# Feed-forward weight transfers kept in program order, each gate and up set issued one group ahead, the first down tiles spread over the last groups

## The chip, the cores and the metric

The kernel runs on one core of one Trainium2 chip. The metric is device time in microseconds (us), the median of several executions. The span of a profile, from its first to its last instruction, is about 1.8 us shorter than the time of the same execution. PE is the matmul engine, DVE the vector engine, ACT the scalar engine, and SP the engine from whose queue the loads are issued.

## The reference

One transformer block with conditioning. The six vectors sa, ca, ga, sb, cb, gb come from `silu(c) @ w_mod`.

```python
h = _layernorm(x, axis=-1) * (1 + ca) + sa
x = x + ga * _A_ref(h, A_k_cache, A_v_cache, A_wq, A_wo)   # attention, 32 heads, last 512 cached keys
h = _layernorm(x, axis=-1) * (1 + cb) + sb
x = x + gb * _B_ref(h, B_w_gate, B_w_up, B_w_down)         # (silu(h@w_gate) * (h@w_up)) @ w_down
```

There are 2048 rows of 1024 values, and the feed-forward width is 3584. Everything is bf16.

## The kernel before

Attention comes first, then the feed-forward part (FFN) in four blocks of 512 rows. A block has seven groups of gate and up products (four units of 16 matmuls each), then two halves of down products. Both kernels hand their instructions to a scheduler, which may reorder each engine's stream by its own estimate. `pin` marks an instruction that it must leave at its place in the program; `stage` says which kinds are pinned. `at(k, ...)` sets a task beside step k.

The names in the views: `xn` is a normalised tile of 128 rows, `hT` holds the transposed rows, which the affine steps then scale and shift. `gu_ps` is the PSUM tile (PSUM is where matmuls accumulate) of one gate and up unit, `sg` the silu of its gate half, and `guT` the product of the two halves; once `guT` is done, the `gu_ps` buffer is free. `d_ps`, `a_ps`, `q_ps` and `s_ps` are the PSUM tiles of the down, output, query and score products. `wg`, `wu` and `wd` are weight tiles; `v_sb` is also the spare weight buffer.

```python
    pb_ = ctx.enter_context(tc.tile_pool(name="blkB", bufs=7))    # gate and up tiles, 512 KB each
    pc_ = ctx.enter_context(tc.tile_pool(name="blkC", bufs=12))   # wo and down tiles
    ...
    stage = {"dma": True, "steps": False}

    def pin(ins, what="steps"):
        return tc.keep_in_program_order(ins) if stage[what] else ins

    def fetch(out, in_):
        pin(nc.sync.dma_start(out=out, in_=in_), "dma")
    ...
    def load_cols(n, k, dst, add_one):           # scale and shift as columns (modT)
        ...
            fetch(out=dst, in_=src)
        if add_one:
            nc.vector.tensor_scalar(out=dst, in0=dst, scalar1=1.0, scalar2=None, op0=ALU.add)
    ...
    def ln_norm(tt, on_act=False):
        mv = ln.pop(tt)
        n = wk.tile([P, D], BF16, name="xn", tag="xn", bufs=3)
        ...
            pin(nc.vector.tensor_scalar(out=n, in0=xt[tt], scalar1=mv[:, 0:1],
                                        scalar2=mv[:, 2:3], op0=ALU.subtract, op1=ALU.mult))
    ...
    def ln_xpose(key, tt):                       # DMA transpose, hT<-xn, on SP's queue
        ...
        pin(nc.sync.dma_start_transpose(
            out=hT[key][:, :, t * P:(t + 1) * P], in_=xn.pop(tt)), "dma")

    def ln_affine(key, dt, ps, sc, sh, on_act):  # eight of these after the four transposes
        ...
            pin(nc.vector.tensor_scalar(out=hT[key][:, dt, :], in0=ps, scalar1=sc[:, dt:dt + 1],
                                        scalar2=sh[:, dt:dt + 1], op0=ALU.mult, op1=ALU.add))
    ...
    def emit_gu(cc, f):
        ...
        ps = big("gu_ps")                        # two PSUM buffers
        ...                                      # 8 gate and 8 up matmuls
        nc.scalar.activation(out=g, in_=ps[:, 0, :], func=ACT.Silu)
        nc.vector.tensor_tensor(out=guT[(cc, fg)][:, fi, :], in0=ps[:, 1, :], in1=g, op=ALU.mult)
    ...
    stage.update(dma=False, steps=False)         # from here the scheduler orders the loads
    for cc in range(NTC):
        for fg in range(NFG):
            if (cc, fg) != (0, 0):
                load_gu(cc, fg)
            if cc > 0:
                load_wd(cc, 0, fg)
            for fi in range(4):
                emit_gu(cc, 4 * fg + fi)
                run_tasks(NU + 1 + (cc * NFG + fg) * 4 + fi)
        for dh in range(DH):
            if dh > 0 or cc == 0:
                for fg in range(NFG):
                    load_wd(cc, dh, fg)
            for t in range(QT):
                ...
                emit_down(cc, dh, t, (256, 128, 128) if last else (512,))
```

Of the kernel before, what the change touches and what calls it, by code (L numbers as in the profile page):

```python
# [588 lines left out]
def fast_path(ctx, tc, flag, A_x, A_k_cache, A_v_cache, A_wq, A_wo, B_x, B_w_gate, B_w_up,  # L589
# [14 lines left out]
    NTC = S // TCW  # L604
# [7 lines left out]
    NFG = FT // 4  # L612
# [30 lines left out]
    def blkB(name, shape, dt=BF16):  # L643
        return pb_.tile(shape, dt, name=name, tag="B")

    def blkC(name, shape, dt=BF16):
        return pc_.tile(shape, dt, name=name, tag="C")
# [10 lines left out]
    stage = {"dma": True, "steps": False}  # L658
# [7 lines left out]
    def load(out, in_):  # L666
        with nc.allow_non_contiguous_dma(reason="weight slice"):
            fetch(out=out, in_=in_)
# [157 lines left out]
# [3 lines that stand above are left out]
        if on_act:  # L829
            nc.vector.scalar_tensor_tensor(out=mv[:, 3:4], in0=mv[:, 0:1], scalar=-1.0,  # L830
                                           in1=mv[:, 2:3], op0=ALU.mult, op1=ALU.mult)
            nc.scalar.activation(out=n, in_=xt[tt], func=ACT.Identity, bias=mv[:, 3:4],
                                 scale=mv[:, 2:3])
        else:
            pin(nc.vector.tensor_scalar(out=n, in0=xt[tt], scalar1=mv[:, 0:1],
                                        scalar2=mv[:, 2:3], op0=ALU.subtract, op1=ALU.mult))
        return n
# [85 lines left out]
    for t in range(QT):  # L923
        ln_stats(t)
        n = ln_norm(t, t % 2 == 0)
# [128 lines left out]
    def emit_o(g):  # L1054
        cc, h = divmod(g, H)
        kv = h // rep
        if h % 4 == 0:
            oq[(cc, h // 4)] = blkC("oq", [P, QT, 4, Dh])
        for t in range(QT):
            if o_slot["n"] == 0:  # L1060
                o_slot["ps"] = mm("o_ps", (P, SLOTS, VN))
            s_ = o_slot["n"]
            for j in range(WT):
                nc.tensor.matmul(o_slot["ps"][:, s_, :], lhsT=pT[g][:, j, t * P:(t + 1) * P],  # L1064
                                 rhs=v_sb[:, kv, j, 0:VN], start=(j == 0),
                                 stop=(j == WT - 1))
            runs = o_slot["runs"]
            if runs and runs[-1][0] == g:
                runs[-1][2] = t + 1
            else:  # L1070
                runs.append([g, t, t + 1, s_])
            o_slot["n"] = s_ + 1
            if o_slot["n"] == SLOTS or (t == QT - 1 and h % HQ == HQ - 1):
                close_bank()
        del pT[g]
# [46 lines left out]
    for tt in range(QT, S // P):  # L1122
        cc, t = divmod(tt, QT)
# [33 lines left out]
    def load_gu(cc, fg):  # L1157

        for nm, v in (("wg", wg_v), ("wu", wu_v)):
            for i in range(2):  # L1160
                spare = (cc * NFG + fg) % 2 == 1 and nm == "wu" and i == 1
                t = v_blk if spare else blkB(nm, [P, 4, 512])
                load(t, v[:, 4 * i:4 * i + 4, fg * 512:(fg + 1) * 512])
                gu_w[(cc, fg, nm, i)] = t

    def emit_gu(cc, f):
        fg, fi = divmod(f, 4)
        if fi == 0:
            guT[(cc, fg)] = blkA("guT", [P, 4, TCW])
        ps = big("gu_ps")  # L1170
        for n, nm in enumerate(("wg", "wu")):
            for dt in range(DT):
                nc.tensor.matmul(ps[:, n, :],  # L1173
                                 lhsT=gu_w[(cc, fg, nm, dt // 4)][:, dt % 4, fi * P:(fi + 1) * P],
                                 rhs=hT[("h2", cc)][:, dt, :], start=(dt == 0),
                                 stop=(dt == DT - 1))
        g = wk.tile([P, TCW], BF16, name="sg", tag="row", bufs=5)
        nc.scalar.activation(out=g, in_=ps[:, 0, :], func=ACT.Silu)  # L1178
        nc.vector.tensor_tensor(out=guT[(cc, fg)][:, fi, :], in0=ps[:, 1, :], in1=g, op=ALU.mult)  # L1179

    def load_wd(cc, dh, fg):
        t = blkC("wd", [P, 4, 512])
        load(t, wd_v[:, 4 * fg:4 * fg + 4, dh * 512:(dh + 1) * 512])
        wd_tiles[(cc, dh, fg)] = t

    def emit_down(cc, dh, t, widths=(512,)):
        row = (cc * QT + t) * P
        c0 = 0
        for w in widths:
            dsl = slice(dh * 512 + c0, dh * 512 + c0 + w)  # L1190
            d_ps = mm("d_ps", (P, w))
            for f in range(FT):
                nc.tensor.matmul(d_ps, lhsT=guT[(cc, f // 4)][:, f % 4, t * P:(t + 1) * P],  # L1193
                                 rhs=wd_tiles[(cc, dh, f // 4)][:, f % 4, c0:c0 + w],
                                 start=(f == 0), stop=(f == FT - 1))
            r = wk.tile([P, w], FP32, name="f32", tag="f32", bufs=2)
            nc.vector.tensor_tensor(out=r, in0=d_ps, in1=gb_bc[:, dsl], op=ALU.mult)  # L1197
            o = wk.tile([P, w], BF16, name="o_sb", tag="row", bufs=5)
            nc.vector.tensor_tensor(out=o, in0=r, in1=xt[cc * QT + t][:, dsl], op=ALU.add)
            nc.scalar.dma_start(out=out2d[row:row + P, dsl], in_=o)  # L1200
            c0 += w

    def run_tasks(k):
        for f, a in tasks.pop(k, ()):
            f(*a)

    stage["steps"] = True
    for k in range(NU + 1):
# [9 lines left out]
        run_tasks(k)  # L1218
        if k >= 1:
            emit_o(k - 1)  # L1220
    stage.update(dma=False, steps=False)
    for cc in range(NTC):
        for fg in range(NFG):
            if (cc, fg) != (0, 0):
                load_gu(cc, fg)
            if cc > 0:
                load_wd(cc, 0, fg)
            for fi in range(4):
                emit_gu(cc, 4 * fg + fi)
                run_tasks(NU + 1 + (cc * NFG + fg) * 4 + fi)  # L1230
        for dh in range(DH):
            if dh > 0 or cc == 0:
                for fg in range(NFG):
                    load_wd(cc, dh, fg)
            for t in range(QT):
                last = cc == NTC - 1 and dh == DH - 1 and t == QT - 1
                emit_down(cc, dh, t, (256, 128, 128) if last else (512,))
# [3 lines left out]
def kernel(tc, *args):  # L1241
    nc = tc.nc
    with tc.tile_pool(name="guard", bufs=1) as gp:
        flag = gp.tile([1, 1], I32, name="flag")
        fast_path(tc, flag, *args)
        over = nc.values_load(flag[0:1, 0:1], min_val=0, max_val=1)
        with tc.If(over > 0):
            general_path(tc, *args)
# [30 lines left out]
```

## Time and profile before

| | |
|---|---|
| time, three runs | 1283.59 us median (1283.0 to 1285.08) |
| time of the profiled run, and its span | 1284.75 us, 1283.0 us |
| PE without a matmul | 13.0 us of the span |
| transfers | 204.21 MB, 159 GB/s over the span |

The prediction below shows the lines that carry its argument. Two more are wanted as a yardstick. They are from the timeline of PE in the kernel before (start, length, engine, line, what): the first gate matmul of the FFN and the first down matmul. The count that ends a line is that of the matmuls merged into it inside the view's window, so a window's end can cut it.

```profile
675.45 1.89 PE L1173 MATMUL gu_ps<-hT,wg 128*128 128x512 bf16 x8
...
793.86 2.32 PE L1193 MATMUL d_ps<-wd,guT 128*128 128x512 bf16 x10
```

Between these two starts lie 28 units of 16 matmuls and 12 output projections of 8, together 544. At the pace of 96.69 / 448 = 0.2158 us they need 117.41 us; the kernel before took 793.86 - 675.45 = 118.41. This stretch holds all that the change can win, while whole executions of one kernel differ by 2 us.

The other small loss in the middle of the kernel lies far from the change, in attention. The waits of PE between 25 and 800 us, in the kernel before (what waited, what for: us in total, times, longest), hold it, beside the gu_ps wait that the prediction shows and two waits for s_ps of 0.3 us each:

```profile
PE a_ps L1096 <- DVE acc L1102: 1.0, 1, 1.0
...
```

A wait in this list is shorter than the hole in the stream. The records give a 512-wide matmul 379 ns, while matmuls follow each other at 216 ns. So the last matmul before a wait "ends" 0.16 us after the next one should have begun. The idle time of 0.83 us at 755.87 is a hole of 0.99 us, and the 1.0 us of a_ps is a hole of 1.15 us.

### The profile page before, as it was taken

What the parts mean: (1) busy time and instruction counts of PE and PEld (TensorE: products, weight loads), DVE (VectorE), ACT (ScalarE), POOL (GpSimd) and SP (SyncE); (2) the same over time, 40 slices, a digit from 0 to 9 for tenths busy, and PEclk for the clock granted to TensorE, in tenths of its full rate; (3) what the DMA queues carried; (4) which work ended last, traced back from release to release, by engine and by line L of the source; (5) the groups of instructions that cost most, each with busy time, mean ns of one, the idle gap of its engine ahead of it and who ended that gap; (6) DMA issues with size and microseconds to landing.
All of it is one profiled execution on the core that took longest, in us unless ns stands there. A gap on an engine that the chain in (4) does not pass through costs nothing.

```text
span 1283.0 us, 18137 instructions
## 1 busy us (share of the span) xinstructions
PE 1270.0 (99%) x7601; PEld 643.1 (50%) x7601; DVE 577.3 (45%) x1271; ACT 333.9 (26%) x433; POOL 1.2 (0%) x8
## 2 busy tenths in 40 slices
PE   8999999999999999999999999999999999999998
PEld 4555555555555555555554444444444444444444
DVE  4464557865577755576663642221212221221122
ACT  3543334343333433333341111011100111011100
POOL 0000000000000000000000000000000000000000
PEclk8999999999999999999999999999999999999999
DMA  9878566557355554445678484454536455454401
GB/s 286 275 187 234 169 149 171 133 142 204 98 124 156 148 140 148 116 149 131 132 195 247 129 249 149 139 189 147 180 103 218 140 164 164 135 193 134 129 22 47
DMA packets 280108, 204.21 MB, mean 159 GB/s; under 512 B 113865, under 2 KB 273609, under 8 KB 280018
## 3 DMA queue, kind: packets, MB, share of 16 engines
q1 hardware_dynamic: 275106, 198.78, 54.1%
q10 hardware_dynamic: 4912, 4.20, 1.0%
q8 instruction: 61, 1.00, 0.3%
q14 instruction: 29, 0.24, 0.1%
HBM read 174.08 MB, written 4.21 MB: 139 GB/s over the span
## 4 chain that ended last, share of the span: by engine, by line
PE 96%; DMA 2%; DVE 1%; SPq 0%; ACT 0%; issue 0%; DVEq 0%
PE gu_ps L1173 29%; PE a_ps L1096 17%; PE q_ps L1019 17%; PE d_ps L1193 15%; PE o_ps L1064 9%; PE s_ps L1032 8%; DMA wm<-in_w_mod_dram 1%; DMA hT<-xn 1%; PE q_ps L940 0%; DMA modT<-row_d 0%; PE row_ps L779 0%; SPq L664 0%; PE mod_ps L753 0%; DVE st L816 0%; ACT pT L1034 0%; PE h_ps L927 0%
## 5 line engine op out<-in xcount | busy, mean ns | idle before, releaser
L1034 ACT ACTIVATE pT<-s_ps 128x1024 bf16<-128x1024 f32 x256 | 248.7, 1020 | 341.8 <-PE s_ps L1032 341.8
L1096 PE MATMUL a_ps<-wo,oT 128*128 128x512 bf16 x1024 | 241.9, 379 | 1.0 <-DVE acc L1102 1.0
L1019 PE MATMUL q_ps<-hT,wq 128*128 128x512 bf16 x1000 | 236.7, 379 | 0.3 <-DVE modT L755 0.3
L1173 PE MATMUL gu_ps<-hT,wg 128*128 128x512 bf16 x896 | 211.7, 379 | 0.8 <-DVE guT L1179 0.8
L1179 DVE TENSOR_TENSOR guT<-gu_ps,sg 128x512 bf16<-128x512 f32 x112 | 77.4, 691 | 282.5 <-ACT sg L1178 282.5
L1178 ACT ACTIVATE sg<-gu_ps 128x512 bf16<-128x512 f32 x112 | 66.9, 597 | 489.6 <-PE gu_ps L1173 438.4
L1193 PE MATMUL d_ps<-wd,guT 128*128 128x512 bf16 (+2 forms) x952 | 194.2, 366 | 0.0
L916 DVE CAST qT<-q_ps 128x512 bf16<-128x512 f32 x128 | 88.2, 691 | 176.9 <-PE q_ps L1019 176.3
L1173 PE MATMUL gu_ps<-hT,wu 128*128 128x512 bf16 x672 | 163.3, 379 | 0.0
L1096 PEld LDWEIGHTS <-oT 128*128 128x128 bf16 x1024 | 99.9, 98 | 122.3 <-issue 2.1
L1019 PEld LDWEIGHTS <-wq 128*128 128x128 bf16 x1000 | 97.8, 98 | 117.8 <-issue 0.3
L1193 PEld LDWEIGHTS <-guT 128*128 128x128 bf16 x952 | 90.9, 98 | 103.0
L1064 PEld LDWEIGHTS <-pT 128*128 128x128 bf16 x2048 | 126.6, 98 | 30.6 <-issue 0.4
L1173 PEld LDWEIGHTS <-wg 128*128 128x128 bf16 x896 | 87.6, 98 | 106.5 <-issue 1.1
L1064 PE MATMUL o_ps<-v_sb,pT 128*128 128x130 bf16 x2048 | 137.1, 220 | 0.0
L1032 PE MATMUL s_ps<-qT,kT 128*128 128x512 bf16 x512 | 131.5, 379 | 0.6 <-ACT pT L1034 0.6
L1173 PEld LDWEIGHTS <-wu 128*128 128x128 bf16 x672 | 65.8, 98 | 79.3
L1051 DVE TENSOR_TENSOR oq<-o_ps,rl 128x256 bf16<-128x256 f32 (+2 forms) x256 | 101.2, 419 | 4.3
L1197 DVE TENSOR_TENSOR f<-d_ps,gb_bc 128x512 f32<-128x512 f32 (+2 forms) x34 | 22.4, 660 | 147.1 <-PE d_ps L1193 147.1
L1104 DVE TENSOR_TENSOR acc<-a_ps,acc 128x512 f32<-128x512 f32 x64 | 44.0, 688 | 38.8 <-PE a_ps L1096 38.8
L1032 PEld LDWEIGHTS <-kT 128*128 128x128 bf16 x512 | 44.9, 98 | 31.7 <-issue 1.3
L1173 PE MATMUL gu_ps<-hT,v_sb 128*128 128x512 bf16 x224 | 57.5, 379 | 0.0
(77 smaller groups left out, 372.6 us busy)
## 6 DMA issues: line engine op xcount, KB each, us to landing
wq<-in_A_wq_dram SPq DMA_DIRECT2D x64, 512.0 KB, 4.2
wo<-in_A_wo_dram SPq DMA_DIRECT2D x64, 512.0 KB, 5.7
wg<-in_B_w_gate_dram SPq DMA_DIRECT2D x56, 512.0 KB, 4.5
wd<-in_B_w_down_dram SPq DMA_DIRECT2D x56, 512.0 KB, 7.1
wu<-in_B_w_up_dram SPq DMA_DIRECT2D x42, 512.0 KB, 5.9
wmr<-in_w_mod_dram SPq DMA_DIRECT2D x8, 1024.0 KB, 11.5
v_sb<-in_B_w_up_dram SPq DMA_DIRECT2D x14, 512.0 KB, 6.2
x<-in_A_x_dram SPq DMA_DIRECT2D x16, 256.0 KB, 5.7
```

The costliest lines, as they stand in the source:

```text
L916: nc.vector.tensor_copy(out=t, in_=q_ps)
L1019: nc.tensor.matmul(q_ps, lhsT=wq_tiles[(cc, h // 4, dt // 4)][:, dt % 4, (h % 4) * P:(h % 4 + 1) * P], rhs=hT[("h1", cc)][:, dt, :], start ...
L1032: nc.tensor.matmul(s_ps[:, i, :], lhsT=kT[:, kv, j * P:(j + 1) * P], rhs=qT[g], start=True, stop=True)
L1034: nc.scalar.activation(out=p[:, 2 * jj:2 * jj + 2, :], in_=s_ps, func=ACT.Exp, scale=scale)
L1051: nc.vector.tensor_tensor(out=dst, in0=ps[:, s0:s0 + cnt, 0:Dh], in1=sc, op=ALU.mult)
L1064: nc.tensor.matmul(o_slot["ps"][:, s_, :], lhsT=pT[g][:, j, t * P:(t + 1) * P], rhs=v_sb[:, kv, j, 0:VN], start=(j == 0), stop=(j == WT - 1))
L1096: nc.tensor.matmul(a_ps, lhsT=oT[(cc, 2 * q + i)][:, hh % 4, t * P:(t + 1) * P], rhs=wo_tiles[(cc, q, dh, i)][:, hh % 4, :], start=(hh == ...
L1104: nc.vector.tensor_tensor(out=acc[(cc, t)][:, dsl], in0=a_ps, in1=acc[(cc, t)][:, dsl], op=ALU.add)
L1173: nc.tensor.matmul(ps[:, n, :], lhsT=gu_w[(cc, fg, nm, dt // 4)][:, dt % 4, fi * P:(fi + 1) * P], rhs=hT[("h2", cc)][:, dt, :], start=(dt ...
L1178: nc.scalar.activation(out=g, in_=ps[:, 0, :], func=ACT.Silu)
L1179: nc.vector.tensor_tensor(out=guT[(cc, fg)][:, fi, :], in0=ps[:, 1, :], in1=g, op=ALU.mult)
L1193: nc.tensor.matmul(d_ps, lhsT=guT[(cc, f // 4)][:, f % 4, t * P:(t + 1) * P], rhs=wd_tiles[(cc, dh, f // 4)][:, f % 4, c0:c0 + w], start=( ...
```

## The change

Its intent: the scheduler no longer orders the FFN's loads. They are issued where the program has them, each gate and up set a group before it is used, and the first block's down tiles with the last four groups in place of one burst at the block's end.

```diff
-    stage.update(dma=False, steps=False)
+    stage.update(steps=False)
     for cc in range(NTC):
         for fg in range(NFG):
-            if (cc, fg) != (0, 0):
-                load_gu(cc, fg)
+            n = cc * NFG + fg + 1
+            if n < NTC * NFG:
+                load_gu(*divmod(n, NFG))
             if cc > 0:
                 load_wd(cc, 0, fg)
+            elif fg >= NFG - 4:
+                for i in range(2):
+                    if 2 * (fg - NFG + 4) + i < NFG:
+                        load_wd(0, 0, 2 * (fg - NFG + 4) + i)
             for fi in range(4):
...
         for dh in range(DH):
-            if dh > 0 or cc == 0:
+            if dh > 0:
                 for fg in range(NFG):
                     load_wd(cc, dh, fg)
```

## The prediction

> **What bounds the kernel now.** I read the page's busy shares first, then the waits of the TensorE alone, then the chain that ended last, then the order of time around the one gap that lies where the change acts.
>
> ```profile
> span 1283.0 us, 18137 instructions
> PE 1270.0 (99%) x7601; PEld 643.1 (50%) x7601; DVE 577.3 (45%) x1271; ACT 333.9 (26%) x433; POOL 1.2 (0%) x8
> ```
>
> PE has 13.0 us without a matmul in the whole span. "Busy" need not mean "at full pace", so the pace has to be checked. In the chain, merged in order of time, the FFN reads:
>
> ```profile
> 745.04 4.90 DMA hT<-xn
> 750.61 3.11 DMA hT<-xn
> 755.87 38.15 PE gu_ps L1173 x176
> 794.02 48.35 PE d_ps L1193 x224
> 842.37 96.69 PE gu_ps L1173 x448
> 939.06 48.35 PE d_ps L1193 x224
> ```
>
> 448 matmuls in 96.69 us is 0.2158 us each, and 224 in 48.35 us is the same. The windows view gives PE 96.60 us busy of 96.60 for 842.4 to 939.0. From 755.87 on, the FFN is one unbroken run of matmuls at one pace, and it waits for no transfer. What is left to win is the idle time. By windows of the span, 5.2 us of the 13.0 lie in the first 25 us, 5.4 us after the last matmul, and 2.4 us between 25 and 800. The waits that the change can reach are listed by the waits view of 675 to 1283 for PE, which has a single line:
>
> ```profile
> PE gu_ps L1173 <- DVE guT L1179: 0.8, 1, 0.8
> ```
>
> Its story in order of time (start, length; in brackets the idle time before it and its releaser):
>
> ```profile
> 750.03 0.55 DVE L835 TENSOR_SCALAR xn<-x,mvl 128x1024 bf16<-128x1024 bf16 x1 [3.51 <-DMA hT<-xn]
> 750.50 0.68 DVE L1179 TENSOR_TENSOR guT<-gu_ps,sg 128x512 bf16<-128x512 f32 x1
> 753.84 1.38 DVE L856 TENSOR_SCALAR hT<-hT,modT 128x512 bf16<-128x512 bf16 x4 [2.66 <-DMA hT<-xn]
> 755.14 0.68 DVE L1179 TENSOR_TENSOR guT<-gu_ps,sg 128x512 bf16<-128x512 f32 x1
> ...
> 755.87 1.89 PE L1173 MATMUL gu_ps<-hT,wg 128*128 128x512 bf16 x8 [0.83 <-DVE guT L1179]
> ```
>
> The last LayerNorm needs four DMA transposes (hT<-xn). DVE is stopped twice for them, before the fourth xn and before the affine step on hT. Behind those stand the guT products that free the two gu_ps banks. PE runs out of banks: the run of 16 matmuls that began at 751.42, each half 1.73 us apart, should have been followed at 754.88 and was at 755.87. That is 0.99 us, the only loss in the FFN.
>
> **What the Trainium skill says.** "TensorE: Matmul & The Clock Gate", section "Back-to-back issue gap", gives N/2.4 + 2.5 ns for one warm matmul, 215.8 ns at N = 512. The trace agrees to the digit. The same section gives 131 ns as the sustained figure for such streams; nothing in this trace comes near it, so the measured 215.8 is the pace that I use, and no better feeding can raise it. "DMA: Bandwidth & Descriptors", section "Queues, rings and completion order", says that on each DMA engine descriptors are consumed in ring order. That is why a small transpose stands behind weights issued earlier on the same queue: the trace shows 4.90 us from issue to landing for the first hT, with eight 512 KB tiles issued since 733.49, and 3.11 us for the last. "Perfetto Trace Analysis", section "Tensor Engine Instruction (MATMUL, LD_WEIGHTS)", calls DVE strict FIFO, and the four lines above show it: a guT whose operands are ready waits behind an xn and an hT.
>
> **The change part by part.** No arithmetic is added or removed, and the built order of PE instructions is the same before and after. Only the order of transfers on the SP queue, and with it the order of a few DVE instructions, moves.
>
> *Gate and up sets.* A set is four 512 KB tiles; seven buffers (and a spare in v_sb for odd sets) hold two sets. So set n+1 can be issued only when group n-1 has released its tiles, whatever the program says. Before does that: for instance 853.62 to 856.6, as group 7 ends at 856.0. Issuing it "one group ahead" waits for the same release. Gain 0. Margin: during a burst the windows view shows 341 to 377 GB/s in 2 us slices, first bytes some 2.2 us after the issue, so a set takes about 2.2 + 2.1 MB / 0.35 = 8.2 us; it is needed 13.8 + 2.4 = 16.2 us after its issue.
>
> *Down tiles.* Before, 14 are issued in a row from the second down phase's tail (30.53 us from 813.04), hoarded for the next block. After, one follows each set: 2.6 MB per group of 13.8 us, about 2.2 + 7.5 = 9.7 us (estimate from the same rate). It fits, and as the tile stands behind the set it delays nothing that is needed sooner. The two tiles that reuse buffers of the first half of the down phase still come 19.2 us into it and are needed at 24.2 + 5 x 0.86 = 28.5 us. But now the next set stands behind them in program order: set 8 goes out at about 814 where it went at 791.46. It is needed at 856, so 34 us remain. For the same reason the fourth hT transpose leaves at about 818.
>
> *Order on DVE.* This is the part that pays. In the built order the fourth xn now follows nine more guT, and the eight affine steps on hT move out of the gate/up groups into the down phase, behind the fifth d_ps product. There PE has four PSUM buffers of 6.05 us work each, so a DVE wait of a few us (hT lands at about 828, DVE is there at about 826) costs nothing. The 0.99 us gap goes: 1283.59 - 0.99 = 1282.60.
>
> *What could take its place.* Three new spots. (1) The fourth xn needs a buffer that the first hT transpose frees. That transpose now stands behind set 6 and two down tiles, 3.15 MB from 762.8: landed at about 762.8 + 2.2 + 9.0 + 1 = 775. DVE reaches xn at 773.7, waits 1.3 us, and is through at 775.6; the next guT is due at 776.4 and PE needs it by 779.1. No loss, with 2.8 us to spare. (2) The score-bound check (gd_d, gd_row, flag) now follows the last oT transposes, so gd_row lands at about 688.5 to 690.5 where it did at 663.7, and DVE waits for it right after the second guT (685.6). Its 3 us of small steps and an acc end at about 691.5 to 693.5, guT follows; PE needs its bank at 696.17. No loss, some 2 us to spare. (3) SP waits for the flag until then, so set 2 goes out about 2 us late, some 14 us before it is spent. I put a quarter of a chance on about 1 us lost in the first two together: +0.2. Sum: 1282.8 us.
>
> **Rivals.** *A real gain from better prefetch* (some 10 us or more): the change's own intent. Against it stands the single PE wait of 0.8 us in 608 us of FFN; there is nothing for a transfer to shorten. At the very best, with all idle time of 25 to 800 us gone too, it would be 1281. *The program order blocks the queue:* SP runs in order, so one waiting transfer holds all behind it; if a set came 5 us late in each block, four blocks would cost 20 us (1303). For it: set 8 and its like now stand behind down tiles that wait for the down phase. Against it: each margin above is at least 5 us for weights. *The new DVE waits bite:* each can cost 1 to 3 us, giving 1283 to 1286; the margins of 2 to 3 us are estimates, so this is the most likely way to be wrong.
>
> **Range and chances.** The three runs before lie within 2.1 us (1283.0 to 1285.08), as large as the effect. Best case -1 us and a low run, 1281.6; worst likely case one new 2 us wait, 1285.2. A change of 2% is 25.7 us: no gain of that size exists in 13 us of idle time, and a loss of that size needs the blocked queue in several blocks.
>
> **What the changed profile would show.** Right: PE's waits after 675 us no longer hold gu_ps on guT at about 755; the eight hT affine steps sit at about 826 to 832; set 8 is issued at about 814; the chain is one PE run through the FFN; busy time stays 1270. Wrong: a PE wait for gu_ps on guT near 696 or 779, or a PE wait for wg, wu or wd at the start of any group or down phase.

## The result, and the profile after

Ratios here are the mean time of one kernel's runs over that of the other's of the same rounds, so not quite the ratio of the medians that are quoted beside them.

| | before | after |
|---|---|---|
| median, six runs each | 1284.17 us (1283.0 to 1285.14) | 1283.48 us (1283.05 to 1285.36) |
| ratio, 95% interval | | 0.9997 (0.9984 to 1.001) |
| first gate matmul to first down matmul | 118.41 us | 117.42 us |
| first gate matmul to the end of the last down matmul | 602.18 us | 601.19 us |

By the clock of whole runs the two kernels are the same. The trace says more. In the first view of the changed kernel, its page, something has to be set aside:

```profile
PE 1262.1 (99%) x7461; PEld 642.4 (50%) x7601; DVE 577.9 (45%) x1271; ACT 333.9 (26%) x433; POOL 1.2 (0%) x8
```

PE seems 8 us less busy. But it has 7601 weight loads and only 7461 matmuls; 140 records are missing from this trace. A second profile of the same kernel (run after_again below) has them all, and its busy time is that of the kernel before:

```profile
PE 1270.5 (99%) x7601; PEld 643.2 (50%) x7601; DVE 577.7 (45%) x1271; ACT 333.9 (26%) x433; POOL 1.2 (0%) x8
```

For questions of idle time I use starts of instructions and that second trace. The place where the hole was, in the timeline of PE of the changed kernel:

```profile
752.51 1.89 PE L1173 MATMUL gu_ps<-hT,wu 128*128 128x512 bf16 x8
754.24 1.89 PE L1173 MATMUL gu_ps<-hT,wg 128*128 128x512 bf16 x8
```

The two starts are 1.73 us apart, eight matmuls at the pace; before, the same two were 755.87 - 753.15 = 2.72 us apart. The list of PE's waits after 675 us, which had one line before, is empty in both profiles of the changed kernel. DVE at the same time and later, in its timeline (in brackets the idle time before, and what ended it):

```profile
755.07 0.69 DVE L1179 TENSOR_TENSOR guT<-gu_ps,sg 128x512 bf16<-128x512 f32 x1 [2.76 <-ACT sg L1178]
...
776.09 0.55 DVE L835 TENSOR_SCALAR xn<-x,mvl 128x1024 bf16<-128x1024 bf16 x1 [3.06 <-DMA hT<-xn]
776.55 0.68 DVE L1179 TENSOR_TENSOR guT<-gu_ps,sg 128x512 bf16<-128x512 f32 x1
...
828.04 2.67 DVE L856 TENSOR_SCALAR hT<-hT,modT 128x512 bf16<-128x512 bf16 x8 [3.98 <-DMA hT<-xn]
```

From 748 us to the end of the block's gate and up products every guT but one now comes at once after its silu (sg); the one behind the fourth xn, at 776.55, is 0.8 us late, which PE does not feel. DVE still stops twice for a transpose, 3.06 us before the fourth xn and 3.98 us before the affine steps, 7.0 us together where it was 6.2 (3.51 and 2.66). But the two stops are 52 us apart and no longer follow each other within one group, and the second lies in the down half, where PE does not need DVE for several us. The price stands in the timeline of SP's queue of the changed kernel (here the length is the time that issuing took):

```profile
767.28 5.11 SPq L848 DMA_TRANSPOSE hT<-xn  x1
...
812.70 1.20 SPq L664 DMA_DIRECT2D wg<-in_B_w_gate_dram  x2
...
818.33 4.44 SPq L848 DMA_TRANSPOSE hT<-xn  x1
```

The second set of the next block (wg at 812.70, set 8 of the prediction) left at 791.46 before; it now stands in program order behind two down tiles that wait for a buffer. Nobody needs it before 854, so this costs nothing. The transposes, which stood at 745 to 751, are now spread from 767 to 818 with weight tiles ahead of them. Their tile's own view, before and then after (issue time min/median/max in ns; us from issue to landing):

```profile
L848 SPq DMA_TRANSPOSE hT<-xn x4: 1232/1289/2382, 745.0 to 750.6; - x4
...
DMA to landing us min/median/max: 3.1/3.2/3.3
```

```profile
L848 SPq DMA_TRANSPOSE hT<-xn x4: 2547/3944/5107, 767.3 to 818.3; - x4
...
DMA to landing us min/median/max: 7.2/8.7/9.6
```

The times to landing count from the start of the issue, and not all four transposes are in them: the fourth xn of the kernel before waited until 750.03 for the first one, issued at 745.04, which makes 4.9 us.

Where did the rest go? The profiled span fell by 1.7 us (1283.0 to 1281.3). 0.99 of it is the hole. 0.64 was there before the FFN began: the first gate matmul started at 674.81 where it was at 675.45. In the second profile of the changed kernel it started at 675.39, and that span is 1.0 us shorter than before, the hole alone. Over the whole FFN, too, the two kernels differ by the hole and by nothing else (602.18 and 601.19 us in the table). So the 0.64 is start-up scatter, so far as two profiles can tell. Over all traces this start lies between 673.89 and 676.14, and the granted clock of the first 25 us between 0.86 and 0.96. That scatter, together with the runs' 2 us, is why a gain of 1 us is invisible in a median of a few runs.

### The profile page after: what moved, and what is told of

It reads as the page before. It is cut to its first block, busy times and chain, and to the rows that moved or that the text cites. A ratio compares the mean times of both kernels' runs of the same rounds, so it can differ in the third digit from the quotient of the medians. Undisturbed runs are those within 1.5% of the kernel's fastest.

```text
span 1281.3 us, 17945 instructions
## 1 busy us (share of the span) xinstructions
PE 1262.1 (99%) x7461; PEld 642.4 (50%) x7601; DVE 577.9 (45%) x1271; ACT 333.9 (26%) x433; POOL 1.2 (0%) x8
## 2 busy tenths in 40 slices
DMA packets 280108, 204.21 MB, mean 159 GB/s; under 512 B 113865, under 2 KB 273609, under 8 KB 280018
## 4 chain that ended last, share of the span: by engine, by line
PE 96%; SPq 2%; DMA 1%; issue 1%; DVE 0%
PE gu_ps L1173 30%; PE a_ps L1096 17%; PE q_ps L1019 16%; PE d_ps L1193 15%; PE o_ps L1064 9%; PE s_ps L1032 8%; SPq L664 1%; SPq L703 1%; DMA modT<-row_d 0%; DMA wq<-in_A_wq_dram 0%; PE row_ps L779 0%; DVE st L816 0%; SPq L848 0%; DVE qT L916 0%; DVE acc L1102 0%
```

## The experiments

My theory: the change is worth the 0.99 us hole and nothing else. The hole came from the order of a few DVE instructions around the last LayerNorm, and no weight transfer was ever waited for. The rivals: the transfers as such matter (better prefetch helps, or program order hurts), or the new DVE waits cost what the old ones did.

Four kernels share the runs of the kernel before in a first group (median 1283.85, nine runs), four in a second (1285.03, nine runs), three in a third (1284.48, nine runs); before's own medians differ by 1.2 us between groups. So each kernel is compared only within its group. "Stretch" is the yardstick from above.

| run | median us | ratio to before (95%) | stretch us | lost over 117.41 |
|---|---|---|---|---|
| before | 1283.85, 1285.03, 1284.48 | | 118.41 | 1.00 |
| affine_late | 1282.33 | 0.9986 (0.9972 to 1.0) | 117.41 | 0 |
| pin_only | 1283.27 | 0.9997 (0.9983 to 1.001) | 118.20 | 0.79 |
| ahead_only | 1284.9 | 1.0007 (0.9994 to 1.0021) | 118.18 | 0.77 |
| xn4 | 1284.51 | 0.9999 (0.9986 to 1.0013) | 118.20 | 0.79 |
| both_gaps | 1282.34 | 0.9978 (0.9964 to 0.9991) | 117.42 | 0.01 |
| no_transfers | 1285.65 | 1.0003 (0.999 to 1.0017) | 119.05 | 1.64 |
| bufs6 | 1288.89 | 1.0031 (1.0015 to 1.0046) | 117.86 | 0.45 |
| bufs5 | 1322.44 | 1.0298 (1.0283 to 1.0314) | 123.10 | 5.69 |
| after_again | 1283.59 | 0.9989 (0.9975 to 1.0002) | 117.41 | 0 |
| dve_both | 1282.47 | 0.9982 (0.9969 to 0.9996) | 117.41 | 0 |
| floor | 1282.79 | 0.9985 (0.9971 to 0.9998) | 117.41 | 0 |

(affine_late, pin_only, ahead_only and xn4 are of the first group; both_gaps, no_transfers, bufs6 and bufs5 of the second; the last three of the third. The stretch covers the first block only. From the first gate matmul to the end of the last down matmul it is 602.18 us in before, 601.18 in affine_late, both_gaps, after_again, dve_both and floor, 606.10 in bufs6 and 633.54 in bufs5; in the other four it exceeds 601.18 by what the stretch loses.)

### affine_late: only the DVE order

The kernel before, with its transfers and their order untouched. The guT products and the affine steps are pinned, so that the eight affine steps can't come before their place in the program. In the built kernel they move into the next block, one behind each of eight guT (874 to 899 us in the trace), and nothing moves on SP or PE.

```diff
-            pin(nc.vector.tensor_scalar(out=hT[key][:, dt, :], in0=ps, ...
+            tc.keep_in_program_order(nc.vector.tensor_scalar(out=hT[key][:, dt, :], in0=ps, ...
-        nc.vector.tensor_tensor(out=guT[(cc, fg)][:, fi, :], in0=ps[:, 1, :], in1=g, op=ALU.mult)
+        tc.keep_in_program_order(nc.vector.tensor_tensor(out=guT[(cc, fg)][:, fi, :], ...
```

> The kernel before with one thing moved: guT and the hT affine steps keep program order on DVE, so the eight affine steps of the last LayerNorm leave the groups around 755 us and come one by one in the tenth and eleventh gate/up group (about 877 to 905 us). SP and PE order are those of before. My theory (the only thing the change bought is that DVE no longer waits for a late hT transpose ahead of guT): the 0.83 us PE wait of gu_ps on guT near 755 is gone, the gate/up matmuls from 751.4 on run at 1.73 us per eight, and the time is about 1 us under before (1283 or a little less), as in the changed kernel, although no transfer was reordered. Rival (the order of transfers is what paid): PE wait stays, time as before.

The stretch fell to 117.41 us and PE's waits after 675 us are none. In DVE's timeline the xn still waits:

```profile
750.63 0.55 DVE L835 TENSOR_SCALAR xn<-x,mvl 128x1024 bf16<-128x1024 bf16 x1 [3.41 <-DMA hT<-xn]
...
752.94 0.69 DVE L1179 TENSOR_TENSOR guT<-gu_ps,sg 128x512 bf16<-128x512 f32 x1 [1.16 <-ACT sg L1178]
```

The guT behind this stop began at 751.10 and the next, at 752.94, is on time again. How late may a guT be? On time it starts 0.83 us after the end of its unit's matmuls, as 755.07 - 754.24 above; it takes 0.69; and PE wants the buffer for the unit after the next, one unit of 3.45 us after that end. So it may be 3.45 - 0.83 - 0.69 = 1.93 us late for nothing. Here it was due one unit before 752.94, at 749.49, and was 1.61 late: no hole. In the kernel before, the guT at 755.14 was due 0.83 after 751.42, at 752.25; it was 2.89 late, 0.96 over the limit, and the hole was 0.99. The whole gain of the change is reproduced without touching one transfer.

### pin_only: program order without the new positions

```diff
-    stage.update(dma=False, steps=False)
+    stage.update(steps=False)
```

> Half of the change: the FFN transfers keep program order, but the loads stand where before has them (each set at its own group, the first down tiles after the last group). My theory: issue of a set is decided by the buffers, so this half alone gives the whole effect through the order of DVE: hT affine steps in the down phase, no PE wait near 755, time about 1 us under before (1282.5 to 1283.5). Sets 7 and 8 then go out only about 20 us into the down phase (near 812 us), which still is in time. Rival (the order blocks the queue unless the loads are issued ahead): PE waits for wg, wu or wd show up at the first down phase or at the group after it, some 5 to 20 us lost.

This expectation was partly missed. No wait for weights arose, as the theory said. The hole at 755 went, as expected, but another came six us later. DVE and PE in their timelines:

```profile
760.17 0.55 DVE L835 TENSOR_SCALAR xn<-x,mvl 128x1024 bf16<-128x1024 bf16 x1 [4.98 <-DMA hT<-xn]
760.63 1.47 DVE L1179 TENSOR_TENSOR guT<-gu_ps,sg 128x512 bf16<-128x512 f32 x2
```

```profile
758.85 1.89 PE L1173 MATMUL gu_ps<-hT,wu 128*128 128x512 bf16 x8
761.37 1.89 PE L1173 MATMUL gu_ps<-hT,wg 128*128 128x512 bf16 x8 [0.63 <-DVE guT L1179]
```

Here the fourth xn stands behind four guT, where the changed kernel has nine and the kernel before one. A transpose behind a weight set, issued from 750.88 in 5.70 us, lands 9.2 to 9.4 us after its issue by the tile's view. So this one stop of 4.98 us is enough. The first of the two guT was due at 754.50 + 3.45 = 757.95 (the last one on time stood at 754.50) and was 2.68 late, 0.75 over the limit; PE lost 0.79 us (761.37 where 758.85 + 1.73 = 760.58 was due). The pin moves the hole; that it vanishes in the changed kernel needs the new positions as well.

### ahead_only: the new positions without the pin

```diff
-    stage.update(steps=False)          # of the changed kernel
+    stage.update(dma=False, steps=False)
```

> The other half: loads written one group ahead and the down tiles spread, but transfers not pinned to program order. My theory: the scheduler puts the transfers about where before has them, the built DVE order is that of before around 755 us, and so the PE wait of about 0.8 us for gu_ps on guT stays; time as before (1283.5 to 1284.5). Rival (issuing ahead is what paid): no PE wait, 1 us or more under before.

The scheduler put the loads back to about their old order, and the hole is there again in PE's timeline:

```profile
755.22 1.02 PE L1173 MATMUL gu_ps<-hT,wg 128*128 128x512 bf16 x4 [0.60 <-DVE guT L1179]
```

Issuing a set "one group ahead" in the program does nothing by itself. DVE has the order of before around the hole, with both stops (3.26 and 2.67 us), and the hole is 0.77 us where before had 1.00: two profiles with the same order there can differ by that much.

### xn4: a fourth buffer for xn

```diff
-        n = wk.tile([P, D], BF16, name="xn", tag="xn", bufs=3)
+        n = wk.tile([P, D], BF16, name="xn", tag="xn", bufs=4)
```

> The kernel before with four xn buffers in place of three: the fourth xn no longer waits for the first hT transpose (3.51 us in before). The affine steps still stand before guT and wait for the last transpose, five now ahead of the next guT. Theory: of the two DVE waits the second (affine on hT) sets the PE gap, so it stays: PE waits 0.7 to 1.4 us for gu_ps on guT, time as before within 0.5 us. Rival (the first wait, the xn buffer, sets it): the gap is gone and about 1 us is won.

The first stop is gone, all four xn run in a row. The hole stays at 0.79 us, for the affine steps then wait longer:

```profile
753.35 1.70 DVE L856 TENSOR_SCALAR hT<-hT,modT 128x512 bf16<-128x512 bf16 x5 [3.83 <-DMA hT<-xn]
```

The idle time that the profile lists, 0.63 us, is a little under the lower end that I had written. Taken with affine_late: the stop before the affine steps, with five of them run before the next guT, is enough for the hole, and the stop before xn alone makes none there. What the first stop adds to the second is not shown: without it the hole is 0.79 us, but ahead_only, which has both stops, has 0.77. The cheap-looking repair, one more buffer, is the wrong one.

### no_transfers: nearly all FFN weights not loaded

Wrong (relative error 0.16). From the changed kernel; the first two sets and the first seven down tiles are loaded and used throughout. The transfers fall from 204.21 to 123.97 MB.

```diff
-                t = v_blk if spare else blkB(nm, [P, 4, 512])
-                load(t, v[:, 4 * i:4 * i + 4, fg * 512:(fg + 1) * 512])
+                n = cc * NFG + fg
+                if n < 2:
+                    t = v_blk if spare else blkB(nm, [P, 4, 512])
+                    load(t, v[:, 4 * i:4 * i + 4, fg * 512:(fg + 1) * 512])
+                else:
+                    t = gu_w[(0, n % 2, nm, i)]
...
-        t = blkC("wd", [P, 4, 512])
-        load(t, wd_v[:, 4 * fg:4 * fg + 4, dh * 512:(dh + 1) * 512])
+        if (cc, dh) == (0, 0):
+            t = blkC("wd", [P, 4, 512])
+            load(t, wd_v[:, 4 * fg:4 * fg + 4, dh * 512:(dh + 1) * 512])
+        else:
+            t = wd_tiles[(0, 0, fg)]
```

> Wrong result on purpose: the changed kernel, but only the first two gate/up sets and the first seven down tiles are loaded, every later group uses them again. So nearly all FFN transfers (some 79 MB of 84) are gone. It bounds what any prefetching could win. Theory: nothing waits for them, so the time stays within 1 us of the changed kernel (1282.5 to 1284.5; the built DVE order has the affine steps ahead of guT again, so a gap of up to 1 us near 755 may be back). Rival (hidden waits on transfers, or contention by them, cost PE time): several us faster, 1275 or less.

Not faster, and above the range that I had given: 1285.65 against 1285.03. The reason is on DVE and PE, in their timelines:

```profile
748.53 0.55 DVE L835 TENSOR_SCALAR xn<-x,mvl 128x1024 bf16<-128x1024 bf16 x1 [1.70 <-DMA hT<-xn]
...
754.46 1.71 DVE L856 TENSOR_SCALAR hT<-hT,modT 128x512 bf16<-128x512 bf16 x5 [4.67 <-DMA hT<-xn]
```

```profile
756.82 0.38 PE L1177 MATMUL gu_ps<-hT,wg 128*128 128x512 bf16 x1 [1.48 <-DVE guT L1183]
```

With the loads gone the scheduler puts the affine steps among the guT again, as in the kernel before. The hole is larger than there, 1.64 us. This is a lesson about the experiment: taking transfers out also changed the order on DVE, so the run did not test one thing. It does show that the hole needs no queue of weights. In SP's timeline one down tile is all that stands among the transposes:

```profile
745.35 1.28 SPq L848 DMA_TRANSPOSE hT<-xn  x1
746.73 0.51 SPq L664 DMA_DIRECT2D wd<-in_B_w_down_dram  x1
747.33 4.96 SPq L848 DMA_TRANSPOSE hT<-xn  x3
```

The first transpose let xn go 748.53 - 745.35 = 3.2 us after its issue, where it was 4.9 before, so the stop before xn is shorter (1.70 us for 3.51). The stop before the affine steps is longer (4.67 us for 2.66), and the hole with it.

### floor: the same, with the DVE order repaired

Wrong in the same way; no_transfers with the edits of dve_both (below), so that the order on DVE is not at the scheduler's will.

> Wrong result on purpose: as the run without FFN transfers, with both DVE repairs in it, so that the gap that it showed (1.48 us of gu_ps on guT) does not blur the bound. Theory: PE waits between 25 and 1277 us are 0.6 us (s_ps on pT), time within 0.7 us of the run with both repairs and all transfers: what the FFN's transfers cost is nothing. Rival (transfers cost PE some time that the waits do not show): 2 us or more faster than that run.

1282.79 us against dve_both's 1282.47 in the same rounds, both with a stretch of 117.41 and 601.18 us for the whole FFN. Taking 80 MB of transfers away from a kernel without the two holes saves nothing. This settles the rival that better prefetch had something to win, and the one that the new order of the queue costs something: neither is there.

### bufs6 and bufs5: how much room the buffers leave

The changed kernel with 6 and with 5 buffers for gate and up tiles in place of 7.

```diff
-    pb_ = ctx.enter_context(tc.tile_pool(name="blkB", bufs=7))
+    pb_ = ctx.enter_context(tc.tile_pool(name="blkB", bufs=6))    # bufs5: 5
```

> The changed kernel with six weight buffers in place of seven, so one or two tiles of each set can be issued only as the group before it ends its first tile, about 2.6 us before they are needed less some. Worked out from landing times of 4.3 to 6.1 us and the order of use, the late tile arrives within a few tenths of its use. Theory (prefetch had several us to spare): FFN loses at most 0.3 us per set, 0 to 8 us in all, most likely 0 to 3; time 1282.5 to 1286, with a possible small loss in the attention part, where wq uses the same buffers. Rival (prefetch one full group ahead is needed): 20 us or more lost.

> The changed kernel with five weight buffers: now two or three tiles of each set come late. From landing times of 4.3 to 6.1 us against 2.6 us of lead, I expect 1 to 2.5 us of PE wait per pair of groups, 14 to 35 us in the FFN, and perhaps some in the attention part; time 1297 to 1325. It shows what a kernel looks like that does wait for its weights: PE waits on DMA of wg, wu, v_sb in the FFN groups. If it stays within 3 us of the changed kernel, my reading of when transfers matter is wrong.

The waits of PE after 675 us, first with 6 buffers, then with 5:

```profile
PE gu_ps L1173 <- DMA v_sb<-in_B_w_up_dram: 3.4, 10, 0.5
```

```profile
PE gu_ps L1173 <- DMA v_sb<-in_B_w_up_dram: 12.1, 11, 1.7
PE gu_ps L1173 <- DMA wu<-in_B_w_up_dram: 5.1, 11, 0.9
PE gu_ps L1173 <- DMA wg<-in_B_w_gate_dram: 4.8, 10, 0.6
PE d_ps L1193 <- DMA wd<-in_B_w_down_dram: 3.5, 3, 2.2
```

bufs6 is slower than before by 3.9 us; its time lies above the upper end that I had written. The waits lie inside the 0 to 8 us that I had allowed in all, but above the 0 to 3 that I had called most likely, and the longest, 0.5 us, is above the 0.3 for one set. With the 0.16 us that each wait hides, 3.4 + 10 x 0.16 = 5.0 us of holes (606.10 - 601.18 = 4.9 by the whole FFN), less the 0.99 that the change saves, gives 4.0. bufs5 is slower by 37 us in the median, inside my range. In its profiled run, the fastest at 1316.18, the four lines sum to 25.5 us in 35 waits, or 31.1 us of holes (32.4 by the whole FFN); less 0.99 that is 30.1, against 1316.18 - 1285.03 = 31.2. The other three runs took 6 to 10 us more; what they waited for was not profiled and stays open. So transfers can bound this kernel: seven buffers and the spare are just enough, and from there on earlier issue has nothing to give.

### both_gaps: the other hole as well

The one wait that is left in the middle of the changed kernel is the a_ps of attention. In the kernel before, DVE and then PE, in their timelines:

```profile
92.00 0.17 DVE L802 TENSOR_SCALAR modT<-modT 128x8 f32<-128x8 f32 x1 [3.62 <-DMA modT<-row_d]
...
92.69 0.67 DVE L1102 COPY acc<-a_ps 128x512 f32<-128x512 f32 x1
```

```profile
90.53 1.89 PE L1019 MATMUL q_ps<-hT,wq 128*128 128x512 bf16 x8
93.41 1.89 PE L1096 MATMUL a_ps<-wo,oT 128*128 128x512 bf16 x8 [0.99 <-DVE acc L1102]
```

It is the same pattern: a tiny DVE step (adding one to 1024 scales, 0.17 us) stands early in DVE's stream, waits 3.62 us for a small transfer, and behind it the copy that frees a PSUM buffer is late. The result of the small step is not wanted until much later. So I moved it, in the changed kernel, to a later place:

```diff
-        if add_one:
-            nc.vector.tensor_scalar(out=dst, in0=dst, scalar1=1.0, scalar2=None, op0=ALU.add)
+    def cols_plus1(dst):
+        pin(nc.vector.tensor_scalar(out=dst, in0=dst, scalar1=1.0, scalar2=None, op0=ALU.add))
...
+    at(24, cols_plus1, cb1)
```

> The changed kernel plus one moved DVE instruction: the +1 on the scale columns, which waits 3.6 us on DVE for a small transfer and holds up acc near 93 us (PE waits about 1.0 us there in before, 1.3 us in the changed kernel), is done eight steps later. SP, PE and ACT order are those of the changed kernel. It is the same mechanism in another place, so the theory says: the PE wait of a_ps on acc is gone, PE waits between 25 and 800 us fall to about 0.6 us, time about 1 us under the changed kernel and 2 us under before (1282.0). Rival: another wait takes its place, time as the changed kernel.

The a_ps wait is gone: the list of PE's waits has no such line, and in PE's timeline a_ps follows q_ps at 1.73 us:

```profile
90.80 1.89 PE L1019 MATMUL q_ps<-hT,wq 128*128 128x512 bf16 x8
92.53 1.89 PE L1096 MATMUL a_ps<-wo,oT 128*128 128x512 bf16 x7
```

The ratio of 0.9978 excludes 1. The two holes sum to 0.99 + 1.15 = 2.1 us; the medians differ by 2.7, which is within what rounds scatter.

### after_again and dve_both: is anything owed to the transfers?

after_again is the changed kernel itself, once more. dve_both is the kernel before with the edits of affine_late and of both_gaps together; the order of its loads and of PE is that of before.

> The changed kernel once more, on the chip of the two kernels sent with it, to see whether its 1 us can be told from the noise of whole runs. Theory: 0.5 to 1.5 us under before, PE waits after 675 us empty as in its first profile. An interval of about 0.13% either way may still hold 1.0.

> The kernel before with its transfers untouched (SP, PE and ACT order the same) and two DVE repairs: affine steps of the last LayerNorm late, and the +1 on the scale columns late. Theory: both PE waits (0.8 us of gu_ps on guT near 755, 1.0 to 1.5 us of a_ps on acc near 93) are gone without any change of transfers; about 2 us under before and within 0.5 us of the changed kernel with the +1 moved (1282.3). Rival (order of transfers matters beyond DVE): at least 1 us slower than that one.

after_again: 0.9989 (0.9975 to 1.0002), a second time about 0.9 us below before in the medians (1284.48 to 1283.59) and a second time not clear of 1. dve_both: 0.9982 (0.9969 to 0.9996), 2.0 us below before, for a sum of 2.1. Its windows view shows what is left (stretch of time, its length, then PE busy, then the other engines, the granted clock, the DMA share, GB/s):

```profile
25.00:675.00 650.00, 649.43 (x4563) 356.69 (x4562) 410.82 (x982) 258.78 (x306) 0.00 (x0) 1.00 0.60 162
675.00:800.00 125.00, 125.00 (x581) 56.68 (x580) 51.08 (x92) 16.72 (x28) 0.00 (x0) 1.00 0.65 194
```

Between 25 and 800 us PE is without a matmul for 0.57 us, all of it the two s_ps waits. What remains of idle time is the start and the last 5 us. dve_both and both_gaps beat the kernel before by about 0.2%, with intervals that exclude 1; dve_both does it with two DVE edits and no change to a transfer. Against the changed kernel in the same rounds (after_again) its median is 1.1 us lower, about the size of the a_ps hole; no interval for that.

## Why the prediction was right

**What bounds the kernel.** Right. PE runs at one matmul in 0.2158 us wherever it runs: 544 x 0.2158 = 117.4 is the measured stretch: 117.41 in after_again, affine_late, dve_both and floor, 117.42 in the changed kernel's first profile and both_gaps. The rate of 216 ns that the Trainium skill gives for a single warm matmul held, in "TensorE: Matmul & The Clock Gate", section "Back-to-back issue gap"; its 131 ns for streams appeared in no stretch of any profile that I read.

**The hole.** Right in place and size: 0.99 us predicted, 118.41 - 117.42 = 0.99 measured. That it came from DVE's order was argued in the prediction and is now shown by affine_late.

**The level.** 1282.8 was predicted, 1283.48 measured. The difference between the kernels was predicted as 0.8 (0.99 less 0.2 for risk) and measured as 0.7 and 0.9. The base was off: three runs of before gave 1283.59, six gave 1284.17. The range, made from the scatter of these runs, held, but it would have held with no change at all: the stretch is the test of the prediction, and the range is not.

**Gate and up sets, down tiles.** Right: no gain and no loss. floor shows that even taking them all away gains nothing; bufs6 and bufs5 show that waits would have been visible. Set 8 left at 812.70 (814 predicted), the fourth transpose at 818.33 (818), the affine steps ran at 828.04 (826 to 832), though DVE stood there from 824.06 on and not from 826, and so waited 3.98 us and not 2.

**The fourth xn.** No loss, as predicted, but the margin was mis-sized. The term was "landed at about 762.8 + 2.2 + 9.0 + 1 = 775", with a DVE wait of 1.3 us and 2.8 us to spare. DVE waited 3.06 us and was through with xn at 776.64. guT ended at 776.55 + 0.68 = 777.23. guT starts 0.83 us after its unit's matmuls end (unit start 754.24, guT at 755.07), so the unit in question, six units on, ended at 774.97, and the unit after the next was to begin one unit (3.45 us) later, at 778.42. The spare was 1.2 us. The mis-sized term is the landing: set 6 left at 762.21 and the transpose had landed by 776.09, 13.9 us later, where the sum has 12.2. Those 1.7 us are the longer wait. In this trace the transpose took 5.11 us to issue (the median before is 1.29) and landed 8.7 us after the start of its issue; that the slow issue is what my sum lacked is likely but not tested. pin_only shows the same wait at 4.98 us, and there it did bite. The chance of a quarter for a loss of this kind was not too high.

**Why the transposes wait.** Right as a reading, but not what made the hole. The first transpose landed 4.9 us after its issue in the kernel before, behind weights, and after 3.2 us in no_transfers, with none ahead; behind a whole set it took 7.2 to 9.6 us in the changed kernel and 9.2 to 9.4 in pin_only. That agrees with the rule that I quoted ("DMA: Bandwidth & Descriptors", section "Queues, rings and completion order": descriptors are consumed in ring order). But this delay sits in the first of the two stops, and xn4, which does not have that stop, lost 0.79 us all the same. The transpose that ended the second stop took 3.11 us, among the shortest here: the hole came from the latency of one transpose after another, with DVE standing in it.

**The score-bound check and SP.** Predicted at 688.5 to 690.5, it ran at 686.25, and the guT behind it came at 689.46 with the silu as its releaser, so not late. Set 2 was predicted 2 us late and left at 691.41, where it was 692.05, both 16.60 us after the first gate matmul. Both steps were too gloomy and harmless.

**Busy time.** Predicted to stay at 1270; the first trace has 1262.1 through missing records, the complete second one 1270.5. The chain as one PE run through the FFN can likewise be seen in the second trace only.

## What to carry to other kernels

On an engine that runs strictly in order, an instruction that waits for a transfer and is not wanted soon should stand as late as its user allows, since whatever frees the busy engine's PSUM stands behind it; with two buffers such a product could be 1.93 us late here for nothing, and each us beyond was lost in full. When an engine's stream has no holes, earlier or better ordered transfers are worth nothing, and what such a change does to the time comes from the order that it happens to cause elsewhere. For effects under the scatter of runs, measure the time between two fixed instructions of the bounding engine and compare it with their number times the pace; but take more than one profile before you read a difference between two holes, which was 0.2 us here for the same order on DVE around it.

## What the Trainium skill lacked or had wrong

- "TensorE: Matmul & The Clock Gate", section "Back-to-back issue gap": the sustained figure of 131 ns for N = 512 was not seen. 448 matmuls with a weight load each took 96.69 us, 215.8 ns each, in the kernel before and in after_again; the figure for an isolated matmul is the sustained one here.
- "Perfetto Trace Analysis", section "Identifying the Most-Contended Engine", proposes the busy share of weight loads, beside the share of peak FLOP/s, as a measure of headroom on TensorE. The weight loads' share is 50% here, while in the stretches of the FFN no matmul could have started sooner at the measured pace (117.41 us for 544). It is right that busy time misleads: a record of 379 ns at a pace of 216 hides 0.16 us of each hole.
- No page says how slow a DMA transpose gets when it is issued behind weight tiles on the same queue: 2.5 to 5.7 us of SP's time for one in the changed kernel's first profile and in pin_only, against a median of 1.25 to 1.29 us in the kernel before, affine_late and no_transfers, and 7.2 to 9.6 us to landing against 3.1 to 4.9.
- No page says that a trace's matmul records can be incomplete while its weight-load records are complete (7461 against 7601 here, and busy time 8 us too low); comparing the two counts shows it.
